# Sliding-window attention and a gated FFN on one core: two heads on half tiles of TensorE, division by block transposes, fewer and longer loads, first batch attended as a whole

## The chip, the core and the metric

One Trainium2 chip, of which the program uses one core. A core has a matrix engine (TensorE, PE in the profile, with its weight loads as PEld), a vector engine (VectorE, DVE), a scalar engine (ScalarE, ACT), GpSimd (POOL) and SyncE (SP), which here only issues transfers. Sixteen DMA engines move data between HBM and the on-chip memory SBUF. PE writes its results into PSUM: 128 partitions of eight banks, of 512 fp32 numbers each. Each engine works through its own instructions in order and waits on semaphores for the others. The metric is the device time of the program in microseconds, as the median of three runs.

## The reference

q, k and v are [4 batches, 8 heads, 768 positions, 64], fp32. Every query sees the first four keys (the sink) and the last 128 keys up to its own position. After attention the heads of a token stand side by side (512 numbers), and a gated FFN follows.

```python
scores = scale * np.matmul(q, k.transpose(0, 1, 3, 2))
keep = is_sink | in_window            # pos < 4, or 0 <= row - col < 128
scores = np.where(keep, scores, -1000000000.0)
a = np.exp(scores - max); a = a / (sum(a) + 1e-09)
x = np.matmul(a, v) -> [3072 tokens, 512]
out = (np.maximum(x @ w_gate, 0.0) * (x @ w_val)) @ w_out    # 512 -> 1536 -> 512
```

## The kernel before

All matmuls are bf16 with fp32 sums. The work of attention is cut into units: one batch and a pair of heads (four pairs p to a batch). Keys are laid out in blocks of 128: block j holds keys 124j to 124j+127, and its first four places are overwritten by the sink's keys in blocks 1, 3 and 5, so that a query finds sink and window in two or three blocks. A unit goes through these steps:

- load (L97): k, q and v by separate transfers for each head, with runs of 64 fp32 numbers (256 B).
- cast (L115): fp32 to bf16, on GpSimd except at the start.
- T (L139): six transposes of q and seven of k on PE into one PSUM tile of two banks (q in bank 0, k in bank 1). Then DVE copies q of head 0 to qz (L153), ACT copies k to kT (L154), DVE copies q of head 1 (L156). qz holds each head's q in its own 64 rows and zeros in the other 64, so that S and V can work on 128 rows.
- S (L158), for three groups G0 to G2: matmuls of kT and qz for both heads into two banks (503, 499 and 415 columns a head), Exp on ACT (L167), multiplication with a mask of ones and zeros on DVE (L168).
- V (L170), for two parts of the queries (376 and 392): matmuls of ee with vn, whose columns 64 to 127 are ones, so that row 64 of the result is the sum of the weights. ACT copies rows 0 to 64 to oab (L179).
- norm (L259): the sums go to HBM, come back spread over partitions (L269), DVE takes the reciprocal (L273), they go to HBM again and come back copied to 64 partitions (R, L279). DVE multiplies oab by R into xT (L287), which is x, transposed, in bf16.

The FFN of a block of half a batch (b, c0, n) runs in twelve chunks m (L296): four matmuls give gp, ACT takes the relu into gs (L304), four matmuls give vp, DVE multiplies both into hT (L309). gp and vp come from a pool of three single-bank tiles. ffn2 (L313) multiplies hT with wo, twelve matmuls for 128 tokens into the single-bank tile op, and ACT copies the result to ot, from where it is stored.

The order is written out by hand (L328 to L472). Of batch 0 only the first halves of the queries are attended in front (units P0), then FFN starts. A chunk with what goes with it is called a slot below: stages of attention (T, V part 1 of the unit before, S G0, S G1, S G2, V part 0), the chunk, and a share of the ffn2 matmuls that are due (f2). In the first 18 slots two stages go with a chunk, afterwards one. Loads run on SyncE's queue three units ahead. Weights come in by GpSimd's queue, cast on the way.

Waits aren't written by hand: the language puts them in from what each instruction reads and writes.

Of the kernel before, what the change touches and what calls it, by code (L numbers as in the profile page):

```python
# [14 lines left out]

QCUT = 376
# [3 lines left out]
def kernel(  # L22
# [20 lines left out]

    den_d = nc.dram_tensor("den_tmp", (B, NP, 2 * S), F32, kind="Internal").ap()
    rcp_d = nc.dram_tensor("rcp_tmp", (B, NP, 2 * S), F32, kind="Internal").ap()
# [3 lines left out]
    hpool = ctx.enter_context(tc.tile_pool(name="hp", bufs=2))  # L49
    xpool = ctx.enter_context(tc.tile_pool(name="xp", bufs=2))  # L50
    rpool = ctx.enter_context(tc.tile_pool(name="rp", bufs=2))
    dpool = ctx.enter_context(tc.tile_pool(name="dp", bufs=3))
    outpool = ctx.enter_context(tc.tile_pool(name="outp", bufs=3))
    ps_gv = ctx.enter_context(tc.tile_pool(name="ps_gv", bufs=3, space=bass.MemoryType.PSUM))
    ps_op = ctx.enter_context(tc.tile_pool(name="ps_op", bufs=1, space=bass.MemoryType.PSUM))
    ps_at = ctx.enter_context(tc.tile_pool(name="ps_at", bufs=2, space=bass.MemoryType.PSUM))


    kf = [const.tile([128, 7, 2, 64], F32, name=f"kf{i}") for i in range(2)]
    vf = [const.tile([128, 7, 2, 64], F32, name=f"vf{i}") for i in range(2)]  # L60
    qf = [const.tile([128, 6, 2, 64], F32, name=f"qf{i}") for i in range(2)]
    kn = [const.tile([128, 7, 2, 64], BF16, name=f"kn{i}") for i in range(2)]
    vn = [const.tile([128, 7, 2, 128], BF16, name=f"vn{i}") for i in range(2)]
    qn = [const.tile([128, 6, 2, 64], BF16, name=f"qn{i}") for i in range(2)]
    kT = [const.tile([128, 7, 128], BF16, name=f"kT{i}") for i in range(2)]
    qz = [const.tile([128, 2, S], BF16, name=f"qz{i}") for i in range(2)]
    ee = [const.tile([128, 3, 2, 512], BF16, name=f"ee{i}") for i in range(2)]
    oab_ = [const.tile([65, 2, S], F32, name=f"oab{i}") for i in range(4)]
    sink = const.tile([4, 2, NP, 2, 64], BF16, name="sink")
    wg = const.tile([128, KO, d_ff], BF16, name="wg")  # L70
    wv = const.tile([128, KO, d_ff], BF16, name="wv")
    wo = const.tile([128, FM, d_model], BF16, name="wo")
    ident = const.tile([128, 128], BF16, name="ident")
    msk = const.tile([128, 3, 2, 512], BF16, name="msk")

    class Unit:


        def __init__(self, i, b, p, half):
            self.i, self.b, self.p, self.half, self.s = i, b, p, half, i % 2  # L80
            if half == 0:
                self.js, self.q0, self.n, self.qn, sub = (0, 1, 2), 0, QCUT, 3, p // 2
                self.jo, self.qo, self.zo = 3 * sub, 3 * sub, 384 * sub
                self.qrows, self.qp = 384, 128
            elif half == 1:
                self.js, self.q0, self.n, self.qn = (2, 3, 4, 5, 6), QCUT, S - QCUT, 4
                self.jo, self.qo, self.zo = 0, 0, 0
                self.qrows, self.qp = S - QCUT, 98
            else:
                self.js, self.q0, self.n, self.qn = tuple(range(7)), 0, S, 6  # L90
                self.jo, self.qo, self.zo = 0, 0, 0
                self.qrows, self.qp = S, 128
            self.j5 = [j for j in self.js if j < 6]
            self.a, self.e = self.jo + self.j5[0], self.jo + self.j5[-1] + 1


        def load(self, eng=None, veng=None):  # L97
            eng, veng = eng or nc.sync, veng or eng or nc.sync
            s, a, e = self.s, self.a, self.e
            for en, x, dst in ((eng, k, kf[s]), (eng, q, qf[s]), (veng, v, vf[s])):  # L100
                for h in range(2):
                    src = x[self.b, 2 * self.p + h]
                    if x is q:
                        r = src[self.q0:self.q0 + self.qrows, :].rearrange("(p n) d -> p n d", n=self.qn)
                        en.dma_start(out=dst[0:self.qp, self.qo:self.qo + self.qn, h, :], in_=r)
                        continue
                    r = bass.AP(src.tensor, src.offset + 124 * self.j5[0] * D,
                                [[D, 128], [124 * D, e - a], [1, D]])
                    en.dma_start(out=dst[:, a:e, h, :], in_=r)  # L109
                if x is not q and 6 in self.js:  # L110
                    en.dma_start(out=dst[0:24, 6, :, :],  # L111
                                 in_=x[self.b, 2 * self.p:2 * self.p + 2, 744:768, :].rearrange("h s d -> s h d"))


        def cast(self, what, eng):  # L115
            s, a, e = self.s, self.a, self.e
            cp = eng.tensor_copy
            if what == "q":
                cp(qn[s][0:self.qp, self.qo:self.qo + self.qn, :, :].rearrange("p j h d -> p (j h d)"),  # L119
                   qf[s][0:self.qp, self.qo:self.qo + self.qn, :, :].rearrange("p j h d -> p (j h d)"))  # L120
                return
            w = 0 if what == "k" else 1
            src, dst = (kf[s], kn[s]) if w == 0 else (vf[s], vn[s])
            if w == 0:
                cp(dst[:, a:e, :, :].rearrange("p j h d -> p (j h d)"),
                   src[:, a:e, :, :].rearrange("p j h d -> p (j h d)"))
            else:
                cp(dst[:, a:e, :, 0:64], src[:, a:e, :, :])  # L128
            if 6 in self.js:
                cp(dst[0:24, 6, :, 0:64], src[0:24, 6, :, :])  # L130
            if self.half == 0:
                cp(sink[:, w, self.p, :, :], src[0:4, a, :, :])
            for j in (1, 3, 5):
                if j in self.js:
                    cp(dst[0:4, self.jo + j, :, 0:64],
                       sink[:, w, self.p, :, :] if self.half == 1 else src[0:4, self.jo, :, :])


        def T(self):  # L139
            s, nq = self.s, self.qn  # L140
            ps = ps_at.tile([128, 2, 1024], BF16, name="tps", tag="at")
            w = self.qp * nq
            po = ps[:, 0, 0:w].rearrange("d (n p) -> d n p", n=nq)
            for t in range(nq):
                nc.tensor.transpose(po[:, t, :], qn[s][0:self.qp, self.qo + t, :, :].rearrange("p h d -> p (h d)"),  # L145
                                    ident[0:self.qp, 0:self.qp])
            for j in self.js:
                nc.tensor.transpose(ps[:, 1, j * 128:(j + 1) * 128],  # L148
                                    kn[s][:, self.jo + j, :, :].rearrange("p h d -> p (h d)"), ident[:])
            z0 = self.zo + self.q0  # L150
            d0, d1 = self.js[0], self.js[-1] + 1
            zq = [qz[s][64 * h:64 * h + 64, h, z0:z0 + w].rearrange("d (p n) -> d n p", n=nq) for h in range(2)]
            nc.vector.tensor_copy(zq[0], po[0:64])  # L153
            nc.scalar.copy(kT[s][:, self.jo + d0:self.jo + d1, :].rearrange("p j n -> p (j n)"),  # L154
                           ps[:, 1, d0 * 128:d1 * 128])
            nc.vector.tensor_copy(zq[1], po[64:128])  # L156

        def S(self, g):  # L158
            s = self.s
            gi, lo, hi, segs = SEG[g]  # L160
            ps = ps_at.tile([128, 2, 512], F32, name="sps", tag="at")
            for h in range(2):
                for j, q0, c0, c1 in segs:
                    nc.tensor.matmul(out=ps[:, h, c0:c1], lhsT=kT[s][:, self.jo + j, :],  # L164
                                     rhs=qz[s][:, h, self.zo + q0:self.zo + q0 + c1 - c0], start=True, stop=True)
            x = ee[s][:, gi, :, lo:hi]
            nc.scalar.activation(x, ps[:, :, lo:hi], Act.Exp, bias=0.0, scale=scale)  # L167
            nc.vector.tensor_tensor(x, x, msk[:, gi, :, lo:hi], op=Alu.mult)  # L168

        def V(self, part, oab):  # L170
            s = self.s
            q0, n, segs = VSEG[part]
            ps = ps_at.tile([128, 2, 512], F32, name="ops", tag="at")
            for h in range(2):
                for i, (j, gi, c0, c1, o0) in enumerate(segs):
# [5 lines left out]
    def load_w(c):  # L181
        n = d_ff // 4
        for w, dst in ((moe_w_gate, wg), (moe_w_val, wv)):
            nc.gpsimd.dma_start(out=dst[:, :, c * n:(c + 1) * n],
                                in_=w.rearrange("(ko ki) n -> ki ko n", ki=128)[:, :, c * n:(c + 1) * n])
# [322 lines left out]
```

The softmax here doesn't subtract the row's maximum and nothing guards it: scores larger than these inputs give would overflow.

## Time and profile before

389.09 us (median; 388.46 to 389.14). The profiled execution has a span of 388.4 us.

| engine | busy us | share |
|---|---|---|
| PE | 272.5 | 70% |
| PEld | 163.6 | 42% |
| DVE | 207.7 | 53% |
| ACT | 141.3 | 36% |
| POOL | 83.2 | 21% |

| group | count | busy us | mean ns |
|---|---|---|---|
| L307 vp matmuls | 384 | 83.2 | 342 |
| L301 gp matmuls | 384 | 84.9 | 346 |
| L320 op matmuls | 288 | 77.3 | 384 |
| L309 hT | 96 | 51.2 | 547 |
| L153 and L156 qz | 20 + 20 | 39.8 + 40.0 | 1990, 2000 |
| L168 mask | 52 | 33.8 | 651 |
| L287 xT | 40 | 33.2 | 830 |

A matmul's mean is its time from start to end; matmuls overlap, so counts times means is more than the busy time. 96241 DMA packets move 37.74 MB, and 85692 of them are under 512 B. The rows of 40 digits in the prediction cut the span into 40 slices of 9.7 us: busy share in tenths for an engine, granted clock in tenths for PEclk. A line of the chain gives start, length and what ran. A line of waits gives the waiting engine and line, whom it waited for, the sum in us, how often, and the longest. A line of the windows gives the stretch, its length, the busy time of PE, PEld, DVE, ACT and POOL with counts of instructions, the granted clock, the busy share of the DMA engines and GB/s.

### The profile page before, as it was taken

What the parts mean: (1) busy time and instruction counts of PE and PEld (TensorE: products, weight loads), DVE (VectorE), ACT (ScalarE), POOL (GpSimd) and SP (SyncE); (2) the same over time, 40 slices, a digit from 0 to 9 for tenths busy, and PEclk for the clock granted to TensorE, in tenths of its full rate; (3) what the DMA queues carried; (4) which work ended last, traced back from release to release, by engine and by line L of the source; (5) the groups of instructions that cost most, each with busy time, mean ns of one, the idle gap of its engine ahead of it and who ended that gap; (6) DMA issues with size and microseconds to landing.
All of it is one profiled execution on the core that took longest, in us unless ns stands there. A gap on an engine that the chain in (4) does not pass through costs nothing.

```text
span 388.4 us, 5029 instructions
## 1 busy us (share of the span) xinstructions
PE 272.5 (70%) x1760; PEld 163.6 (42%) x1760; DVE 207.7 (53%) x286; ACT 141.3 (36%) x225; POOL 83.2 (21%) x203
## 2 busy tenths in 40 slices
PE   0245230176384695687498989898988999999996
PEld 0122120045252453444255555454645555555552
DVE  5661230347877767861847575767667544222220
ACT  1233120126343543531353544445363533333331
POOL 6240531307424304311404040404010000000000
PEclk9999999999887878969599999999999999999999
DMA  9957199565684554408074747291211211110002
GB/s 178 146 112 125 37 177 196 121 157 117 131 157 102 124 125 94 119 27 166 1 138 95 137 101 137 59 191 33 68 29 43 71 43 53 39 44 29 27 34 103
DMA packets 96241, 37.74 MB, mean 97 GB/s; under 512 B 85692, under 2 KB 92364, under 8 KB 96216
## 3 DMA queue, kind: packets, MB, share of 16 engines
q1 hardware_dynamic: 87208, 31.91, 37.5%
q0 software_dynamic: 5808, 4.72, 8.0%
q10 hardware_dynamic: 3200, 0.79, 1.0%
q8 instruction: 14, 0.23, 0.3%
q14 instruction: 11, 0.09, 0.1%
HBM read 35.64 MB, written 6.49 MB: 108 GB/s over the span
## 4 chain that ended last, share of the span: by engine, by line
PE 48%; DVE 24%; DMA 11%; ACT 6%; issue 4%; SPq 4%; POOL 1%; DVEq 0%; ACTq 0%; POOLq 0%
PE vp L307 14%; PE op L320 13%; PE gp L301 12%; DVE qz L153 10%; DVE qz L156 8%; PE sps L164 6%; DMA kf<-in_k_dram 4%; ACT kT L154 3%; DMA R<-rcp_tmp 3%; DMA dc<-den_tmp 2%; DVE xT L287 2%; PE ops L176 2%; ACT ee L167 2%; SPq L109 2%; SPq L111 1%
## 5 line engine op out<-in xcount | busy, mean ns | idle before, releaser
L307 PE MATMUL vp<-xT,wv 128*128 128x384 bf16 (+2 forms) x384 | 83.2, 342 | 14.2 <-ACT gs L304 14.2
L301 PE MATMUL gp<-xT,wg 128*128 128x384 bf16 (+2 forms) x384 | 84.9, 346 | 5.9 <-DVE hT L309 4.1
L320 PE MATMUL op<-wo,hT 128*128 128x512 bf16 x288 | 77.3, 384 | 0.0
L309 DVE TENSOR_TENSOR hT<-gs,vp 128x384 bf16<-128x384 f32 (+2 forms) x96 | 51.2, 547 | 43.4 <-PE vp L307 42.4
L164 PE MATMUL sps<-qz,kT 128*128 128x251 bf16 (+5 forms) x232 | 35.3, 293 | 47.8 <-DVE qz L156 39.5
L167 ACT ACTIVATE ee<-sps 128x1006 bf16<-128x1006 f32 (+4 forms) x52 | 46.1, 900 | 53.2 <-PE sps L164 53.2
L304 ACT ACTIVATE gs<-gp 128x384 f32<-128x384 f32 (+2 forms) x96 | 47.2, 492 | 41.4 <-PE gp L301 40.9
L307 PEld LDWEIGHTS <-wv 128*128 128x128 bf16 x384 | 39.2, 102 | 47.6 <-issue 25.9
L168 DVE TENSOR_TENSOR ee<-ee,msk 128x1006 bf16<-128x1006 bf16 (+4 forms) x52 | 33.8, 651 | 39.4 <-ACT ee L167 38.8
L287 DVE TENSOR_TENSOR xT<-oab,R 64x768 bf16<-64x768 f32 (+2 forms) x40 | 33.2, 830 | 34.4 <-DMA R<-rcp_tmp 34.1
L128 POOL CAST vn<-vf 128x768 bf16<-128x768 f32 (+2 forms) x20 | 14.7, 732 | 165.8 <-PE ops L176 163.1
L154 ACT COPY kT<-tps 128x896 bf16<-128x896 bf16 (+2 forms) x20 | 15.6, 778 | 95.1 <-DVE qz L153 95.1
L164 PEld LDWEIGHTS <-kT 128*128 128x128 bf16 x232 | 23.0, 113 | 63.6 <-issue 31.9
L156 DVE COPY qz<-tps 64x768 bf16<-64x768 bf16 (+2 forms) x20 | 40.0, 2000 | 17.1 <-ACT kT L154 17.1
L301 PEld LDWEIGHTS <-wg 128*128 128x128 bf16 x384 | 37.3, 103 | 27.6 <-issue 7.9
L176 PE MATMUL ops<-ee,vn 128*128 128x248 bf16 (+6 forms) x256 | 28.6, 255 | 25.8 <-DVE ee L168 18.1
L153 DVE COPY qz<-tps 64x768 bf16<-64x768 bf16 (+2 forms) x20 | 39.8, 1990 | 7.3 <-PE tps L148 7.2
L320 PEld LDWEIGHTS <-hT 128*128 128x128 bf16 x288 | 28.5, 99 | 25.9 <-issue 1.2
L176 PEld LDWEIGHTS <-vn 128*128 128x128 bf16 x256 | 22.5, 103 | 35.0 <-issue 26.5
L179 ACT COPY oab<-ops 65x752 f32<-65x752 f32 (+1 forms) x32 | 25.4, 795 | 25.5 <-PE ops L176 25.3
L145 PE MATMUL tps<-ident,qn 128*128 128x128 bf16 (+1 forms) x100 | 9.8, 236 | 18.5 <-DVE qn L119 18.3
L324 ACT COPY ot<-op 128x512 f32<-128x512 f32 x24 | 14.1, 587 | 22.2 <-PE op L320 22.2
(47 smaller groups left out, 117.9 us busy)
## 6 DMA issues: line engine op xcount, KB each, us to landing
out_dram<-ot SPq DMA_DIRECT2D x24, 256.0 KB
kf<-in_k_dram SPq DMA_DIRECT2D x24, 192.0 KB
qf<-in_q_dram SPq DMA_DIRECT2D x24, 192.0 KB
vf<-in_v_dram SPq DMA_DIRECT2D x24, 192.0 KB
R<-rcp_tmp SPq DMA_DIRECT2D x12, 384.0 KB
wg<-in_moe_w_gate_dram POOLq DMA_DIRECT2D x4, 384.0 KB, 6.3
wv<-in_moe_w_val_dram POOLq DMA_DIRECT2D x4, 384.0 KB, 8.1
wo<-in_moe_w_out_dram POOLq DMA_DIRECT2D x3, 512.0 KB, 16.3
```

The costliest lines, as they stand in the source:

```text
L153: nc.vector.tensor_copy(zq[0], po[0:64])
L156: nc.vector.tensor_copy(zq[1], po[64:128])
L164: nc.tensor.matmul(out=ps[:, h, c0:c1], lhsT=kT[s][:, self.jo + j, :], rhs=qz[s][:, h, self.zo + q0:self.zo + q0 + c1 - c0], start=True, s ...
L167: nc.scalar.activation(x, ps[:, :, lo:hi], Act.Exp, bias=0.0, scale=scale)
L168: nc.vector.tensor_tensor(x, x, msk[:, gi, :, lo:hi], op=Alu.mult)
L176: nc.tensor.matmul(out=ps[:, h, o0:o0 + c1 - c0], lhsT=vn[s][:, self.jo + j, h, :], rhs=ee[s][:, gi, h, c0:c1], start=i == 0, stop=i == le ...
L287: nc.vector.tensor_tensor(x[64 * h:64 * h + 64, p, q0:q0 + n], oab[0:64, h, q0:q0 + n], R[0][:, h, 0:n], op=Alu.mult)
L301: nc.tensor.matmul(out=gp[:, 0:n], lhsT=wg[:, ko, m * 128:(m + 1) * 128], rhs=x[:, ko, c0:c0 + n], start=ko == 0, stop=ko == KO - 1)
L304: nc.scalar.activation(gs[:, 0:n], gp[:, 0:n], Act.Relu, bias=0.0, scale=1.0)
L307: nc.tensor.matmul(out=vp[:, 0:n], lhsT=wv[:, ko, m * 128:(m + 1) * 128], rhs=x[:, ko, c0:c0 + n], start=ko == 0, stop=ko == KO - 1)
L309: nc.vector.tensor_tensor(hT[:, m, c0:c0 + n], gs[:, 0:n], vp[:, 0:n], op=Alu.mult)
L320: nc.tensor.matmul(out=op, lhsT=hTs[b][:, m, t * 128:(t + 1) * 128], rhs=wo[:, m, :], start=m == 0, stop=m == FM - 1)
```

## The change

The kernel's attention and its order are written anew; chunk and ffn2 do the same matmuls as before. Part by part:

- Loads: k and q of both heads come in one transfer each, with partition p of 96 holding eight neighbouring positions of a head (2 KB runs). v keeps 256 B runs. The weights come in fp32 into three staging buffers wst and are cast by GpSimd. All loads stand on SyncE's queue. This is to need fewer packets[...].
- T: sixteen transposes of 96 columns bring k and q to rows by head and to columns by (n, p), and the copies out of PSUM sort the columns (stride of 96 in PSUM, contiguous in SBUF): DVE 128, ACT twice 248, DVE 144 columns of k, DVE 768 of q, and a small copy of the sink. Head 0 is in rows 0 to 63, head 1 in rows 64 to 127, with no zeros.
- S: the two heads' matmuls use 64 rows each (half tiles). In the front part a matmul of the identity with mb adds -30000 to what is masked out, before Exp, in place of DVE's multiplication.
- V: each head's result goes to 64 columns of its own (half tiles); a second set of matmuls, with ones as weights, gives the sums on all 64 rows. Parts of 384 queries.
- Division: DVE transposes the sums in 32x32 blocks, takes the reciprocal of every 32nd column, transposes it back, spread, and multiplies it with the values in PSUM into xT. The way through HBM is gone.
- Buffers: PSUM is four tiles of two banks. In the front part all four rotate; later PS[2] and PS[3] serve attention, gp and vp rotate over the two halves of PS[0] and the first of PS[1], and op has the second half of PS[1].
- Order: batch 0 is attended as a whole in front. Its 24 slots then take both halves in turn for each m, with two stages a slot from slot 12 on; the 48 slots of batches 1 and 2 take one stage each, and the 24 of batch 3 none. The ffn2 matmuls of a batch run in the slots of the next one, three a slot, and those of batch 3 at the end, on three banks.

The diff, cut to its core:

```diff
-QCUT = 376
+BIG = 30000.0
+CUT = 384
...
+    PS = [pspool.tile([128, 2, 512], F32, name=f"ps{i}") for i in range(4)]
+    GV = [PS[0][:, 0, :], PS[0][:, 1, :], PS[1][:, 0, :]]
...
+    def load_kq(u):
+        for x, dst in ((k, kf[u.i % NQ]), (q, qf[u.i % NQ])):
+            nc.sync.dma_start(out=dst[0:PR, :, :],
+                              in_=x[u.b, 2 * u.p:2 * u.p + 2].rearrange("h (p n) d -> p h (n d)", n=NR))
...
+    def load_w(c, w, dst, i, o):
+        n = 256
+        nc.sync.dma_start(out=wst[i % NW][:, o:o + KO * n].rearrange("p (ko n) -> p ko n", n=n),
+                          in_=w.rearrange("(ko ki) n -> ki ko n", ki=128)[:, :, c * n:(c + 1) * n])
...
+    def T(u):
+        t = u.i % NT
+        ps = nextps()[:].bitcast(BF16)
+        for j, x in ((1, kn[u.i % 2]), (0, qn[u.i % 2])):
+            for n in range(NR):
+                nc.tensor.transpose(ps[:, j, 96 * n:96 * n + 96],
+                                    x[0:PR, n, :, :].rearrange("p h d -> p (h d)"), ident[0:PR, 0:PR])
+        vk, vq = (ps[:, j, 0:768].rearrange("d (b p) -> d p b", p=PR) for j in (1, 0))
...
+        nc.vector.tensor_copy(to(e[:, 0:128]), vk[:, 0:16])
+        for i in range(2):
+            nc.scalar.copy(to(e[:, 132 + 252 * i:380 + 252 * i]), vk[:, 16 + 31 * i:47 + 31 * i])
+        nc.vector.tensor_copy(to(e[:, 636:780]), vk[:, 78:96])
+        nc.vector.tensor_copy(to(qT[t][:]), vq)
...
+    def Sg(u, g, bias=False):
...
+        if bias:
+            for h in range(2):
+                nc.tensor.matmul(out=ps[:, h, 0:n], lhsT=ident[:], rhs=mb[:, g, 0:n], start=True, stop=False,
+                                 skip_group_check=True)
+        for x0, q0, c0, c1 in segs:
+            for h in range(2):
+                nc.tensor.matmul(out=ps[:, h, c0:c1], lhsT=kE[t][64 * h:64 * h + 64, x0:x0 + 128],
+                                 rhs=qT[t][64 * h:64 * h + 64, q0:q0 + c1 - c0], start=not bias, stop=True,
+                                 skip_group_check=True)
...
+    def V(u, part):
+        ps = nextps()
+        segs = VSEG[part]
+        for which in range(2):
+            for i, (j, g, c0, c1, o0) in enumerate(segs):
+                for h in range(2):
+                    w = vn[u.i % NV][:, j, h, :] if which == 0 else ones[:]
+                    nc.tensor.matmul(out=ps[64 * h:64 * h + 64, which, o0:o0 + c1 - c0], lhsT=w,
+                                     rhs=ee[u.i % NE][:, g, h, c0:c1], start=i == 0, stop=i == len(segs) - 1,
+                                     skip_group_check=True)
...
+        nc.vector.transpose(out=t1[:], in_=ps[:, 1, 0:CUT])
+        nc.vector.reciprocal(r[:], t1[:].rearrange("p (c e) -> p c e", e=32)[:, :, 0])
+        nc.vector.transpose(out=R[:].rearrange("p (c e) -> p c e", e=32),
+                            in_=r[:].unsqueeze(2).to_broadcast([128, CUT // 32, 32]))
+        nc.vector.tensor_tensor(xT[u.b % 2][:, u.p, CUT * part:CUT * part + CUT], ps[:, 0, 0:CUT], R[:], op=Alu.mult)
...
+        gp, vp = GV[gvn[0] % 3], GV[(gvn[0] + 1) % 3]
...
+    OP = [[PS[1][:, 1, :]], [PS[1][:, 1, :], PS[2][:, 0, :], PS[3][:, 0, :]]]
...
         for p in range(NP):
+            if p + 1 < NP:
+                head_T(U[p + 1])
+            for g in range(3):
+                Sg(U[p], g, bias=True)
+            cast_v(U[p], nc.gpsimd)
...
             if p >= 1:
+                for part in range(2):
+                    V(U[p - 1], part)
+        for c in range(6):
+            cast_w(c, wg, c, 0, nc.gpsimd)
+            cast_w(c, wv, c, 1024, nc.gpsimd)
+            if c + 3 < 6:
+                load_w(c + 3, moe_w_gate, wg, c + 3, 0)
+                load_w(c + 3, moe_w_val, wv, c + 3, 1024)
+        for part in range(2):
+            V(U[3], part)
+        for u in U[4:7]:
+            load_kq(u)
+            load_v(u)
         for c in range(3):
-            load_wo(c)
-
-
+            load_wo(c, c)
+            cast_wo(c, c, nc.gpsimd)
...
+        def first(i):
+            cast_qk(U[i], nc.gpsimd, nc.gpsimd)
+            cast_v(U[i], nc.gpsimd)
+            T(U[i])
...
+            if s < 24:
+                want.append(max(0, s - 11) * 2)
+            else:
+                want.append(min(len(stages), 24 + (s - 23)))
...
+            chunk(b, g, m)
+            while si < want[s]:
+                stages[si]()
+                si += 1
+            for _ in range(3):
+                if f2:
                     f2.popleft()()
```

## The prediction

> **What bounds the kernel now.** I read the page's engine and clock rows first, then the chain of waits in order of time, the list of waits, and the windows of 20 us.
>
> ```profile
> PE   0245230176384695687498989898988999999996
> PEclk9999999999887878969599999999999999999999
> DMA  9957199565684554408074747291211211110002
> ```
> ```profile
> 50.65 11.72 DMA kf<-in_k_dram
> 77.32 3.48 DMA R<-rcp_tmp
> ...
> 100.19 2.63 DVE qz L153
> 115.72 2.63 DVE qz L153
> 130.12 2.73 DVE qz L153
> 145.20 2.73 DVE qz L153
> ...
> 224.63 2.73 DVE qz L153
> 227.39 0.92 ACT kT L154
> 228.33 2.75 DVE qz L156
> ...
> 242.75 2.64 DVE qz L153
> 345.90 0.65 PE gp L301 x4
> 349.80 0.65 PE gp L301 x4
> ```
> ```profile
> ACT kT L154 <- DVE qz L153: 95.1, 20, 20.6
> PE sps L164 <- DVE qz L156: 39.5, 17, 5.7
> DVE qz L156 <- ACT kT L154: 17.1, 20, 1.0
> ```
> ```profile
> 0.00:20.00 20.00, 2.85 (x18) 1.88 (x18) 12.35 (x39) 3.53 (x5) 8.65 (x26) 1.00 0.89 157
> 340.00:360.00 20.00, 20.00 (x115) 11.06 (x113) 5.62 (x11) 6.09 (x12) 0.00 (x0) 1.00 0.09 33
> ```
> Four stretches. To 82 us PE is nearly idle: the chain runs over small loads and the den_tmp/rcp_tmp round trip. From 82 to about 200 two attention stages fall into a slot (one chunk plus what goes with it), and a unit takes 15 us (115.72 - 100.19, and so on)[...]. From 200 to 314 a unit takes 17.9 us (six slots). From 314 PE is full at 1.95 us a slot (two slots from 345.90 to 349.80: chunk 2 x 0.65, three op matmuls 0.65). In a unit the same three copies always stand on the chain: 2.73 + 0.92 + 2.75 = 6.4 us from PSUM to the S matmuls. The third fence says that ACT's copy, which reads the tile's second bank, waits for VectorE's reading of the first, and VectorE's second for ACT. PE does the next slot meanwhile and then idles: a unit's PE work is 6 x 1.95 + 3.1 (S and V 2 x 2834 columns, T 13 x 128, at 384 columns in 0.163 us) = 14.8 of 17.9 us.
>
> [...]the readers of two banks of one tile went one after the other, 20 times of 20.[...]
>
> **Part by part.**
> *Loads.* Runs of 256 B moved 157/0.89 = 176 GB/s of busy engines, 23 ns a packet; the 2 KB stores of the last stretch 33/0.09 = 367 GB/s, 89 ns; between them 1 KB comes to 51 ns (estimate). A unit had 4704 packets of 256 B (6.8 us over 16 engines). Now k and q are 384 of 2 KB (2.1 us), v 1584 of 256 B (2.3): 4.4 us. A weight pair is 1024 x 51/16 = 3.3 us, a third of wo 2.8. The den/rcp transfers and R's 6 MB go. One consequence is a new wait: on GpSimd the wo casts stand ahead of the casts of unit 4, and SyncE sends wo behind units 0 to 6 and all weights: 7 x 4.4 + 6 x 3.3 + 3 x 2.8 = 59 us, with start and landing 63, with casts **67 us: no T of unit 4 before**. Behind it on PE is all of FFN from slot 12.
>
> *T.* 16 transposes of 96 columns. Reading hops 192 B in PSUM, writing is contiguous: DVE 128, ACT 2 x 248, DVE 144, DVE 768 elements, one after the other if the readers stay tied. Bounds: [...]3.5 (before's strided writing, 2724/768) gives 6.0. [...]**3.4 us, from 6.4**.
>
> *Division.* Each half: [...]reciprocal 0.2 (222 ns), [...]multiplication 0.55 (as hT, 547): 1.8 us of DVE, 3.7 a unit; bounds 3.2 and 5. It replaces two xT (1.95), one reciprocal and the ACT copies of oab (1.6), and waits for no DMA. Per unit DVE has some 3.3 (T with ACT's share) + 2.0 (masks) + 3.7 + 3.3 (hT) = 12 us: below a unit's time, so not the bound with one stage a slot.
>
> *PE.* V doubles its matmuls (36; ones give the sum in 64 rows), S halves its rows. Weight loads in a tight run take about 0.055 us (seven in 0.43 at 223.99), so a concurrent pair can't take under 0.11: T 0.9 + S 7 x 0.11 + V 18 x 0.11 = 3.7 us. With no concurrency: 0.9 + 1.2 + 2.6 = 4.7. I take 4.2, and 1.0 (0 to 1.5)[...]. So attention costs PE 5.2 a unit instead of 3.1.
>
> *Steady slots.* 6 x 1.95 + 5.2 = 16.9; between T and S lie op (0.65) and a chunk (1.3), so of 3.4 us 1.4 shows: **18.3 a unit, against 17.9**: the gain on T is spent on V.
>
> *Two-stage slots* (12 to 23): before's 15 us less 3.0 (T) plus 1.5 (DVE division on the chain) = 13.5 a unit.
>
> *Head.* First T at about 7 us (setup, loads). Period by DVE: q cast 0.5, T 1.2 + 3.4, V and two divisions 4.6, about 10 us; four units and the last division: **first chunk at 45 us instead of 82**. The bias matmuls (PE) lie under the T copies, the table load that the warm activation pulls forward (1.3 us) under the first loads, the weight casts (18 on GpSimd, about 1.2 us each after 0.89 for 768 elements) under the landing of the next weights. This, not the steady state, is the gain.
>
> *Banks.* gp, vp and op were tiles of their own. Now two of the three gp/vp banks share tile PS0, and the third shares PS1 with op. If order is kept per tile, as T shows it for readers, vp waits in one slot of three for the relu of gp in the other bank (0.2 + 0.49 = 0.7 us), and in one of three op waits for hT (0.75, hidden where a stage lies between). That is 0.28 a slot with stages, 0.55 without.
>
> **The sum and the rivals.**
> A, halves tied: 45; 12 slots to 67 (with tie or wait for unit 4); four units 4 x 13.5 + 3 = 57, to 124; 48 slots 8 x 18.3 + 48 x 0.28 = 160, to 284; 24 x 2.5 = 60, to 344; last op 72 x 0.215 + 3 = 18.5: **362**. For it: three copies tied 20 times of 20. Against: those are readers; no writing into one half during reading of the other occurs in before.
> B, halves free: 67 + 54 + 146 + 47 + 18.5 = **333**.[...]
> C, slower: hopping reads at 3.5 ns add 2.6 us a unit: 4 x 2 in the head, 4 x 2.6, 8 x 2.6 = 39 onto A: **401**. For it: VectorE's strided writes did cost that.
> D: [...]pairs fully concurrent, free halves: steady units 11.7 + 3.7 + 0.4 = 15.8 (-20), the rest -8: **305**.[...]
>
> **How the numbers follow.** A 0.45, B 0.27, C 0.18, D 0.10. I predict A, 362. The range 318 to 398 holds A, B and edges of C and D. Of C nearly all is above 389.9: slower 0.18, same 0.02, faster 0.80.
>
> **What would show it.** First gp near 45 us; first T of unit 4 near 67, after the casts of wo; [...]under waits, vp for gs and op for hT with 10 us and more in total (A) or none (B); steady units of 18 to 20 us; S and V pairs that start together. Wrong if loads arrive much later than 63 us[...], or if GpSimd's casts fall behind and T waits for them in every unit.

## The result, and the profile after

The changed kernel takes **358.9 us** (median of four runs; 357.96 to 360.7), 389.12 before (four runs): a ratio of 0.923, with a 95% interval of 0.9195 to 0.9264. The forecast was 362 us. Times below are medians of all runs, while ratios leave out runs in the slower state, of which the kernels at 321.0 and 300.5 us have one each (without it 319.8 and 299.3; the trace of the first is of that run). The line numbers in this part are those of the new kernel: T's copies L178 to L183, S matmuls L196, V matmuls L213, division L219 to L223, gp L235, relu L238, vp L240, hT L242, op L255, ot L259, GpSimd's casts of k and q L111 and of wo L129.

The rows of PE and DMA, in slices of 8.9 us, on the page of the kernel after:

```profile
PE   1868287655965888898888889897989788878895
DMA  8999999399560005107230520000000000000032
```

PE is at work from the first slices on, and DMA is done with the bulk by slice 12. But PE never gets to a long row of nines, not even in the last quarter, where it was full before. The first gp matmul starts at 41.7 us; before, at 79.0 (its fourth waited until 82.0, the number that the forecast used). So the front gained 37 us, while from there to the end the new kernel takes longer: 314.6 us (356.3 - 41.7) against 309.4 (388.4 - 79.0), though it has less attention left to do. The change won once and gives back a little afterwards.

The chain of waits after, around the first T behind the front, and then at the T of three steady units:

```profile
68.48 1.04 POOL wo L129
69.52 0.98 POOL kn L111
70.50 0.99 POOL qn L111
...
71.55 0.53 PE ps L172 x8
...
73.39 0.86 DVE qT L182
...
125.66 0.70 PE ps L172 x16
144.72 0.70 PE ps L172 x16
163.28 0.70 PE ps L172 x16
```

The casts of wo stand in front of those of unit 4, as forecast. The steady units are 18.6 to 19.1 us apart (144.72 - 125.66, and so on); over seven units the mean is 18.8. The three copies of 2.73, 0.92 and 2.75 us of before are gone from the chain; q's takes 0.86 there.

The waits of PE after (engine and line, whom it waited for, us in all, times, longest):

```profile
PE ps L240 <- ACT gs L238: 20.7, 32, 0.9
PE ps L196 <- DVE qT L182: 13.8, 12, 3.3
PE ps L255 <- DVE hT L242: 8.9, 16, 0.7
...
PE ps L235 <- ACT ot L259: 4.1, 6, 0.7
PE ps L235 <- DVE hT L242: 3.5, 5, 0.7
```

PE's waits for T's last copy of q (qz L156 before, qT after) are down from 39.5 to 13.8 us. Four others now cost 37.2 us together. vp (L240) waits for the relu in 32 slots of 96, one in three: it has no use for the relu's result, and only writes into the other bank of the tile that the relu reads. The same goes for op on hT and gp on ot and hT: the hT that op multiplies is that of the batch before, and has long been done.

### The profile page after: what moved, and what is told of

It reads as the page before. It is cut to its first block, busy times and chain, and to the rows that moved or that the text cites. A ratio compares the mean times of both kernels' runs of the same rounds, so it can differ in the third digit from the quotient of the medians.

```text
span 356.3 us, 5404 instructions
## 1 busy us (share of the span) xinstructions
PE 276.0 (77%) x2114; PEld 148.3 (42%) x2136; DVE 173.6 (49%) x348; ACT 116.0 (33%) x202; POOL 71.9 (20%) x90
## 4 chain that ended last, share of the span: by engine, by line
PE 59%; DVE 16%; ACT 8%; issue 5%; DMA 5%; SPq 2%; POOL 2%; ACTq 0%; DVEq 0%; POOLq 0%
PE ps L255 17%; PE ps L240 15%; PE ps L235 14%; PE ps L213 5%; PE ps L196 4%; DVE hT L242 4%; ACT gs L238 4%; DVE qT L182 3%; PE ps L172 3%; DMA wst<-in_moe_w_out_dram 3%; DMA vf<-in_v_dram 2%; ACT kE L180 2%; ACT ot L259 2%; DVE R L221 2%; DVE t L219 2%
## 5 line engine op out<-in xcount | busy, mean ns | idle before, releaser
L242 DVE TENSOR_TENSOR hT<-gs,ps 128x384 bf16<-128x384 f32 x96 | 53.1, 553 | 104.9 <-PE ps L240 104.4
L240 PE MATMUL ps<-xT,wv 128*128 128x384 bf16 x384 | 81.9, 337 | 21.5 <-ACT gs L238 20.7
L235 PE MATMUL ps<-xT,wg 128*128 128x384 bf16 x384 | 82.6, 339 | 14.4 <-DVE xT L223 6.8
L238 ACT ACTIVATE gs<-ps 128x384 f32<-128x384 f32 x96 | 47.1, 491 | 127.3 <-PE ps L235 126.4
L255 PE MATMUL ps<-wo,hT 128*128 128x512 bf16 x266 | 71.4, 380 | 10.1 <-DVE hT L242 8.9
L240 PEld LDWEIGHTS <-wv 128*128 128x128 bf16 x384 | 38.5, 100 | 56.8 <-issue 35.9
L200 ACT ACTIVATE ee<-ps 128x1006 bf16<-128x1006 f32 (+2 forms) x48 | 45.1, 961 | 40.7 <-PE ps L196 40.7
L235 PEld LDWEIGHTS <-wg 128*128 128x128 bf16 x384 | 37.4, 100 | 50.3 <-issue 21.8
L111 POOL CAST kn<-kf 96x1024 bf16<-96x1024 f32 x16 | 16.6, 1035 | 115.8 <-PE ps L172 112.7
L255 PEld LDWEIGHTS <-hT 128*128 128x128 bf16 x288 | 25.0, 97 | 35.3 <-issue 13.9
L202 DVE TENSOR_TENSOR ee<-ee,msk 128x1006 bf16<-128x1006 bf16 (+2 forms) x36 | 25.2, 700 | 28.6 <-ACT ee L200 28.4
L196 PE MATMUL ps<-qT,kE 64*128 64x251 bf16 (+4 forms) x224 | 21.7, 281 | 16.5 <-DVE qT L182 13.8
L196 PEld LDWEIGHTS <-kE 64*128 64x128 bf16 x224 | 10.5, 101 | 35.4 <-issue 30.0
L259 ACT COPY ot<-ps 128x512 f32<-128x512 f32 x24 | 14.0, 583 | 27.3 <-PE ps L255 24.2
L219 DVE STREAM_TRANSPOSE t<-ps 128x384 f32<-128x384 f32 x32 | 18.6, 580 | 5.9 <-PE ps L213 4.8
L221 DVE STREAM_TRANSPOSE R<-r 128x384 f32<-128x384 f32 x32 | 18.5, 578 | 1.1
L223 DVE TENSOR_TENSOR xT<-ps,R 128x384 bf16<-128x384 f32 x32 | 17.8, 557 | 1.1
L213 PE MATMUL ps<-ee,vn 128*64 128x255 bf16 (+8 forms) x288 | 16.1, 236 | 0.9 <-DVE xT L223 0.9
L213 PEld LDWEIGHTS <-vn 128*64 128x64 bf16 x288 | 12.5, 110 | 7.6 <-issue 7.2
L213 PE MATMUL ps<-ee,ones 128*64 128x255 bf16 (+8 forms) x288 | 15.6, 233 | 0.0
```

Of the source, the lines that this page charges most:

```text
L196: nc.tensor.matmul(out=ps[:, h, c0:c1], lhsT=kE[t][64 * h:64 * h + 64, x0:x0 + 128], rhs=qT[t][64 * h:64 * h + 64, q0:q0 + c1 - c0], start ...
L200: nc.scalar.activation(x, ps[:, :, 0:n], Act.Exp, bias=0.0, scale=scale)
L202: nc.vector.tensor_tensor(x, x, msk[:, g, 0:n].unsqueeze(1).to_broadcast([128, 2, n]), op=Alu.mult)
L213: nc.tensor.matmul(out=ps[64 * h:64 * h + 64, which, o0:o0 + c1 - c0], lhsT=w, rhs=ee[u.i % NE][:, g, h, c0:c1], start=i == 0, stop=i == l ...
L219: nc.vector.transpose(out=t1[:], in_=ps[:, 1, 0:CUT])
L221: nc.vector.transpose(out=R[:].rearrange("p (c e) -> p c e", e=32), in_=r[:].unsqueeze(2).to_broadcast([128, CUT // 32, 32]))
```

## The experiments

Each time is beside runs of the kernel before on the same chip (389.5 to 390.0 us); a ratio is to that kernel, with its 95% interval. All but one kernel start from the changed one (0.923).

**One bank to a tile.**

```diff
-    PS = [pspool.tile([128, 2, 512], F32, name=f"ps{i}") for i in range(4)]
-    GV = [PS[0][:, 0, :], PS[0][:, 1, :], PS[1][:, 0, :]]
...                                       # PS[2], PS[3] stay; PS[0], PS[1] are given back after the front
+        headps.__exit__(None, None, None)
+        one = [single.tile([128, 512], F32, name=f"one{i}") for i in range(4)]
+        GV += [one[i][:] for i in range(3)]
+        OP += [[one[3][:]], [one[3][:], PS[2][:, 0, :], PS[3][:, 0, :]]]
```

> The changed kernel, with gp, vp and op each in a PSUM tile of one bank after the head (same seven banks of use, same order of work, same instructions). Theory (two banks of one tile are kept in order): the waits vp<-gs (20.7 us, 32 times), op<-hT (8.9) and gp<-hT (3.5) go. Of the 2.5 us of a batch 3 slot 0.5 goes (24 slots, -12), of a steady unit's 18.8 us about 2.2 (8 units, -17); slots 0 to 11 get shorter but the T of unit 4 still waits for GpSimd's casts at 70.5, so nothing there. Together 329 us (322 to 337). Rival (the ties only stand where PE would wait anyway, for ACT's relu or VectorE's queue): 355 to 360, with other waits in the place of these.

Measured: **321.0 us**, ratio 0.821 (0.817 to 0.826), 38 us less than the changed kernel. Its largest wait of PE, in the first fence, and its timeline of PE at the end of slot 11 in the second (start, length, engine, line, what; in brackets the idle time ahead and who ended it; here gp is L238, vp L243, T L175):

```profile
PE ps L175 <- POOL kn L114: 18.5, 3, 11.4
```
```profile
59.41 0.81 PE L238 MATMUL one<-xT,wg 128*128 128x384 bf16 x4
60.05 0.81 PE L243 MATMUL one<-xT,wv 128*128 128x384 bf16 x4
72.28 0.82 PE L175 MATMUL ps<-ident,kn 96*128 96x96 bf16 x8 [11.41 <-POOL kn L114]
```

No wait of vp for the relu, or of op for hT, is left. Four matmuls follow four at 0.65 us, from the first slots on. A steady unit takes 16.2 us instead of 18.8, a slot of batch 3 1.95 instead of 2.65 (in the kernel after, the gp of its first and last slot start at 273.12 and 334.12, 23 slots apart). The banks and matmuls are the same; what went is an order that is kept between the two halves of one tile. The twelve slots ahead of unit 4 got shorter for nothing: PE then stands 11.4 us for GpSimd.

**The casts of wo behind, and batch 1 spread.**

```diff
             load_wo(c, c)
-            cast_wo(c, c, nc.gpsimd)
...                                       # in first(i), ahead of T(U[i])
+            if i == 6:
+                for c in range(3):
+                    cast_wo(c, c, nc.gpsimd)
...
-                want.append(max(0, s - 11) * 2)
+                want.append(min(24, max(0, s - 3) * 6 // 5))
```

> The changed kernel, same instructions, with two placements changed: GpSimd's casts of wo stand behind the casts of units 4 to 6 instead of ahead of them, and batch 1's 24 stages are spread over slots 4 to 23 instead of two a slot over slots 12 to 23. Theory (the T of unit 4 waits only for GpSimd's queue, its data being there by about 46, and two-stage slots run at the pace of a chain, 13.5 us a unit with PE 60 to 75% busy): T of unit 4 at 49 to 53 instead of 70.6, slots 4 to 23 at 2.6 to 2.9 us each, batch 1's start at 104 to 110 instead of 125: 337 to 345 us. Rival (a unit takes its 13.5 us however it is spread, and the clock of this stretch falls further): 351 to 360.

> The untied kernel with the same two placements changed. There PE stood 11.4 us for the casts of unit 4 ahead of its T, and two-stage units took 13.4 to 14.5 us. Theory (ties, GpSimd's order and the chain of two stages a slot are three separate costs): 291 to 300 us. Rival (only the wait for the casts goes; the two-stage stretch is bound by something that moves along, clock or VectorE): 308 to 312.

Measured: with the ties **345.1 us**, ratio 0.887 (0.882 to 0.892); without them **300.5**, 0.770 (0.766 to 0.775). The first T of unit 4 came at 53.7 and 50.7 us instead of 70.6 and 72.3. 14 us of the changed kernel were GpSimd's order and the two stages a slot, and 20 of the untied one: with the ties, the costs nearly add up (38 + 14, of 58 together). Each theory came out ahead of its rival, but at the upper end of its range or just past it: 345.1 and 300.5 us where 337 to 345 and 291 to 300 were expected, and with the ties T of unit 4 at 53.7 (49 to 53) and of unit 8 at 112.0 (104 to 110). The two placements were not tried apart. In the changed kernel PE stood only 0.8 and 0.5 us for GpSimd's casts at the T of unit 4 (11.4 in the untied one), so there the order of the casts alone could bring little: it is what lets the stages start earlier.

**T one stage ahead.** On top of both:

```diff
+            if i % NP == 0:
                 order.append(stage_T(i))
...
+            if i % NP < NP - 1:
+                order.insert(len(order) - 1, stage_T(i + 1))
```

> The untied kernel with wo's casts behind and batch 1 spread, and with the T of a batch's next unit one stage earlier, ahead of the second V of the unit before it. Theory (what is left in slots 4 to 23 is PE's wait for T's copies, 2.35 us in three of four units, and some 3 us in the steady part; a slot's chunk and V are then in between): 290 to 294 us. Rival (the clock and VectorE's queue eat it: another wait of the same size on hT or xT takes its place): 298 to 302.

Measured: **289.1 us**, ratio 0.742 (0.738 to 0.745). The waits on qT were 11.0 us in the version before this; now PE's largest wait for T's copies is:

```profile
PE ps L199 <- DVE qT L185: 2.1, 3, 1.0
```

This is the fastest kernel of the study: 70 us under the changed one, with the same instructions on every engine.

**Halves: heads one after the other, and both heads on one half.**

```diff
-        for x0, q0, c0, c1 in segs:
-            for h in range(2):
+        for h in range(2):
+            for x0, q0, c0, c1 in segs:      # S; in V likewise
```
```diff
-                    nc.tensor.matmul(out=ps[64 * h:64 * h + 64, which, o0:o0 + c1 - c0], lhsT=w,
+                    nc.tensor.matmul(out=ps[0:64, which, o0:o0 + c1 - c0], lhsT=w,   # S: rows 0:64 for both heads
```

> The changed kernel, with the matmuls of the two heads in S and V issued one head after the other instead of alternating, so that no two neighbours stand on different halves of PE (but for one boundary per group). Theory (neighbours on different halves run at the same time): V's 16 and 20 matmuls go from 0.71 and 0.83 us to 1.1 and 1.3 (2572 and 3096 columns at 384 in 0.163), S gains 0.5: +1.4 us a unit on a PE that is the bound in 12 of 16 units, 371 to 380 us. Rival (the time is in the weight loads and the number of matmuls, not in concurrency): 0.71 and 0.83 stay, 357 to 361.[...]

> The changed kernel with both heads of S and V on the same half of PE: head 1's scores are computed from head 0's rows, and its V lands on head 0's 64 output rows, so head 1's attention is not computed. Same number and size of matmuls, but no two on different halves. Theory (halves run at the same time whether neighbours alternate or follow one another, which is why the kernel with heads one after the other lost only 4 us): V's 16 and 20 matmuls take 1.1 and 1.3 us instead of 0.71 and 0.83, S 1.2 instead of 0.7: 1.4 us a unit, 375 to 381 us. Rival (the pace is set by the number of matmuls, 0.044 us each, whatever half they stand on): 357 to 361.

Measured: heads one after the other 362.9 us, ratio 0.929 (0.926 to 0.933): neither theory's number. Both on one half **395.7**, 1.016 (1.012 to 1.019). The two V parts of a unit on PE, in the kernel after and then with both heads on one half:

```profile
156.02 0.81 PE L240 MATMUL ps<-xT,wv 128*128 128x384 bf16 x4
156.76 0.47 PE L213 MATMUL ps<-ee,vn 128*64 128x255 bf16 x8
157.09 0.45 PE L213 MATMUL ps<-ee,ones 128*64 128x255 bf16 x8
157.47 0.82 PE L255 MATMUL ps<-wo,hT 128*128 128x512 bf16 x2
```
```profile
162.97 0.77 PE L213 MATMUL ps<-ee,vn 128*64 128x255 bf16 x8
163.60 0.75 PE L213 MATMUL ps<-ee,ones 128*64 128x255 bf16 x8
164.28 0.82 PE L255 MATMUL ps<-wo,hT 128*128 128x512 bf16 x2
```

From the first matmul to what follows, the same sixteen take 0.71 us on two halves (157.47 - 156.76) and 1.31 on one. So the halves did run at the same time. With one head after the other they took 0.73: what came next on the free half did not have to stand next in the program (at the end of the values there, the first matmul of the sums starts at 163.33 us on one half, ahead of the last of the values, 163.38, on the other). So that order was no test of concurrency, and my expectation of 1.1 us was wrong. A steady unit went from 18.8 to 20.4 us on one half, about the 1.4 us expected. Of the 37 us in all, though, some 18 lie ahead of the first gp (59.5 instead of 41.7). PE ran at half pace there until 27 us and again from 36 to 47 (V's first sixteen matmuls took 2.4 us at 23.61, and 1.2 at 50.09), and in between it stood 7.9 us for VectorE's cast of q, which took 5.87 us instead of 0.69. Why the pace stayed low and the cast was slow isn't settled.

**k and q in 256 B runs.**

```diff
-                              in_=x[u.b, 2 * u.p:2 * u.p + 2].rearrange("h (p n) d -> p h (n d)", n=NR))
+            for h in range(2): ... in_=x[u.b, 2 * u.p + h].rearrange("(n p) d -> p n d", n=NR))
...
-        vk, vq = (ps[:, j, 0:768].rearrange("d (b p) -> d p b", p=PR) for j in (1, 0))
+        vk, vq = ps[:, 1, 0:768].rearrange("d (p b) -> d p b", b=8), ps[:, 0, 0:768]
```

> The changed kernel, with k and q loaded in runs of 256 B again (96 rows apart, one transfer a head, same queue), which brings the columns out of T in natural order, so T's copies then read PSUM without hops. Theory (loads set the head and the T of unit 4): 2.4 us more for each of seven units (from 4.4 to 6.8 by 23 ns a packet), first gp at 46 to 52 instead of 41.7, T of unit 4 at 80 to 87 instead of 71; 368 to 376 us in all. Rival (the transfers lie beside weight casts and PE work): 357 to 361. T's 768-element copy: 0.95 us as now if the hop in PSUM costs nothing, less if it does.

Measured: **356.7 us**, ratio 0.916 (0.912 to 0.920), so no slower than the changed kernel. The loads do come later: the first gp at 44.1 us (41.7), the first T of unit 4 at 77.1 (70.6), 6.5 us of the 9 to 16 expected. T paid it back. Its q copy with the hop, after, and without:

```profile
L182 DVE COPY qT<-ps x16: 947/948/949, 9.2 to 259.1; 128x768 bf16<-128x768 bf16 x16
```
```profile
L182 DVE COPY qT<-ps x16: 545/547/550, 9.6 to 260.4; 128x768 bf16<-128x768 bf16 x16
```

The hop of 192 B costs VectorE 0.40 us in 768 elements (1.23 against 0.71 ns each, fixed costs included); ScalarE's 248 took 369 ns either way. A steady unit took 18.0 us instead of 18.8. The 2 KB runs, together with the hop that they bring into T's copies, gained nothing in the end. They were one of the change's four points.

**Sorting on the read side: alone on the kernel before, and undone in the changed one.**

```diff
-        zq = [... .rearrange("d (p n) -> d n p", n=nq) for h in range(2)]       # the kernel before
+        zq = [... .rearrange("d (p n) -> d p n", n=nq) for h in range(2)]
+        po = po.rearrange("d n p -> d p n")
```
```diff
-        nc.vector.tensor_copy(to(qT[t][:]), vq)                                 # the changed kernel
+        nc.vector.tensor_copy(qT[t][:].rearrange("d (p b) -> d b p", b=8), ps[:, 0, 0:768].rearrange("d (b p) -> d b p", p=PR))
```

> The kernel before with one thing changed: the two qz copies of T read PSUM with the hop and write SBUF in order, instead of reading in order and writing with a step. Theory (the step on the write side is what made T's chain 6.4 us, and the chain stands on the path of every unit): each copy goes from 2.72 to about 0.95 us, the chain to 2.8; two-stage units from 15 to 12-12.5 (8 units), steady ones from 17.9 to 15.5-16.5 (6): 345 to 357 us, so as good as the whole change. Rival 1 (something else takes the chain's place: the round trip of den_tmp, PE itself): 372 to 386. Rival 2 (hopping reads cost what stepped writes cost): 389.

> The changed kernel with one part of it undone: T's q copy reads PSUM in order and writes SBUF with a step of 16 B (the four k copies stay sorted). Theory (a stepped write costs 3.5 ns an element, and T's copies stand on the path): the copy goes from 0.95 to about 2.7 us, and the 1.75 us show in twelve of sixteen units and partly in the head: 378 to 384 us. Rival (op and a chunk lie between T and its S matmuls, 1.95 us of PE work, so most is hidden): 359 to 366.

Measured: two lines of the kernel before alone give **364.2 us**, ratio 0.934 (0.931 to 0.938), 26 us of the whole change's 30, and with no shorter front (first gp at 77.3 instead of 79.0). The copies fell from 2.73 to 0.95 us, a steady unit from 17.7 to 15.7. It stayed 7 us above my range, and part of the gain went to another wait. The largest of PE in that kernel, V's wait for the mask, was 18.1 us in 4 waits before the edit, and five of the eight now stand in the two-stage stretch, with 8.6 us:

```profile
PE ops L177 <- DVE ee L169: 27.7, 8, 12.7
```

Undone in the changed kernel, **405.3 us**, ratio 1.040 (1.033 to 1.046): 46 us more, twice what the theory said and slower than before. The timeline of PE there, at the S matmuls of a steady unit:

```profile
150.63 0.60 PE L197 MATMUL ps<-qT,kE 64*128 64x255 bf16 x4 [2.91 <-DVE kE L184]
151.16 1.46 PE L256 MATMUL ps<-wo,hT 128*128 128x512 bf16 x3
152.42 1.40 PE L236 MATMUL ps<-xT,wg 128*128 128x384 bf16 x4
153.65 0.81 PE L241 MATMUL ps<-xT,wv 128*128 128x384 bf16 x4
```

The copy took 3.55 us, not 2.7 (4.6 ns an element at a step of 16 B; 3.5 at before's 12 B). Nearly all of the 2.6 us more show in the wait (2.91 against 0.30 and 0.26 after). And PE comes back slow: three op and four gp matmuls take 1.26 and 1.23 us from start to start, where the same seven took 0.65 and 0.66 at 145.60 us, ahead of the wait. The granted clock was 0.52 from 151.2 to 153.7 us, and 1.00 from there to 157; in the kernel after it was 1.00 from 147 to 154. A unit lost 3.7 us (22.5 against 18.8). Of the 48.5 us between the two profiled spans, 26 lie in the steady units, 10 between the T of units 4 and 8, and 11 ahead of the first gp (53.0 instead of 41.7).

**The way through HBM, for all of batch 0 and for one unit.** The sums go to den_tmp, come back, their reciprocals go to rcp_tmp and come back as R, by four transfers on ScalarE's queue:

```diff
+        if u.b == 0:              # in the second kernel: if u.i == 3
+            trip(u, part, ps, t1, R)
+            return
```

> The changed kernel with the division of batch 0 alone undone: sums go to DRAM, come back as 96 rows of 8, the reciprocals go out and come back broadcast over 64 partitions (on ScalarE's queue, each step issued one stage after the one before); batches 1 to 3 keep the block transposes. Theory (the round trip is what stood last before the first chunk in the kernel before): the first gp at 52 to 62 instead of 41.7, and the end later by what the cast-bound T of unit 4 leaves (slots 0 to 11 have about 1 us to spare): 368 to 380. Rival (the head is bound by its loads and weight casts, the round trip lies beside them): first gp at 42 to 46, 358 to 363.

> The changed kernel with the round trip through DRAM for the division of one unit alone, the last of batch 0 (both its halves; ScalarE's queue, nothing else queued behind). Tells what one trip adds where nothing stands in a line. Theory (a trip is four transfers of 2 to 7 us each, as the trips of all four units showed, against 1.95 us of VectorE): first gp at 53 to 60 instead of 41.7, the end later by that less about 1 us: 367 to 378. Rival (the trips cost only because they stood in a line for two buffers): first gp below 48, 358 to 363.

Measured: **413.6 us**, ratio 1.062 (1.057 to 1.066), with all four units; **376.4**, 0.967 (0.962 to 0.972), with one. With all, that is far above the 368 to 380 expected, and the first gp had its fourth matmul only at 102.1 us (52 to 62 expected): trips stood in a line for two buffers (ScalarE's copies wait 22.1 us for the xT that frees one) and in ScalarE's queue, where Exp stands behind the transfers, so that number is an upper end. With one, the first gp had its fourth matmul at 55.7 us, as expected, and the chain of waits shows the price (the first line is the first half's transfer, the others are the second half's):

```profile
38.93 4.97 DMA den_tmp<-R
...
45.66 2.12 DMA den_tmp<-R
...
47.87 3.68 DMA dc<-den_tmp
...
51.81 3.95 DMA rcp_tmp<-dr
...
56.32 6.19 DMA R<-rcp_tmp
...
62.64 0.57 DVE xT L238
```

24.7 us lie between the first sums (37.92) and the last xT, for what VectorE does in 3.9 (two halves of 1.95). Some 7 of them (45.66 - 38.93) are a line here too: ScalarE copies the second half only when the first half's sums have landed, because its queue already holds their next transfer. The first half alone took 17.2 us, to its xT at 55.10. The first T of unit 4 came 18 us later, the end 17.5.

## Why the prediction was right, and where it was right by luck

| step | forecast (A) | after | tiles untied |
|---|---|---|---|
| first gp, us | 45 | 41.7 | 42.5 |
| first T of unit 4 | 67 | 70.6 | 72.3 |
| first T of unit 8 | 124 | 125.5 | 128.1 |
| steady unit | 20.0 with the tie | 18.8 | 16.2 |
| slot of batch 3 | 2.5 | 2.65 | 1.95 |
| last op matmuls to the end | 18.5 | 20.0 | |

The forecast's terms add up to 362.5. With what was measured in their place the sum closes: 362.5 + 1.5 (unit 8) - 12.4 (the steady stretch, from there to the first gp of batch 3, took 147.6, not 160) + 3.2 (batch 3 took 63.2, not 60) + 1.5 (end) = 356.3, the profiled span. That 362 came so near is in part luck: errors named below cancel.

**Ties (case A against B): right.** The waits stood where and as often as forecast, one slot in three. Untied, the kernel went to 321 us, beyond B's 333. I had put 29 us on the ties; they cost 38. In the steady part it was 2.6 us a unit instead of 1.7, because there too vp's wait shows nearly in full beside stages, and in batch 3 it was 0.7 us a slot instead of 0.55: 8 x 2.6 + 24 x 0.7 = 37.6.

**Head: right, for the reason given first.** "45 instead of 82" was 41.7 instead of 79.0. One trip through HBM kept in one unit takes 17.5 us of that back. The loads' part of the argument was priced too high: by "6.8 to 4.4 us a unit", at 23 ns a packet, twice the packets should have cost the first gp 4 to 10 us and the T of unit 4 9 to 16. They cost 2.4 and 6.5, and with T's cheaper copies the end came no later.

**GpSimd's queue: right.** wo's casts ahead of unit 4's, T at 70.6. That this was not forced, and cost 14 us together with the two-stage slots, the forecast didn't see.

**Steady slots: near by luck, four terms mis-sized and partly cancelling.** PE's attention was put at 5.2 us a unit, of which 1.0 was my estimate for ten changes between full and half tiles, not shown in the trace of before, and 4.2 for T and for pairs half concurrent. On top came 1.4 for what shows of T and 1.7 for the tie. In the untied trace a unit leaves 16.2 - 6 x 1.95 = 4.5, of which 0.6 is PE's waits for T's copies. T takes 0.68 us, S about 1.0 and V 1.54. So PE's attention is 3.9 and what shows of T 0.6, and the tie was 2.6: 20.0 - 1.3 - 0.8 + 0.9 = 18.8. My estimate of 0.11 us as the floor for a pair, from two weight loads of 0.055 one after the other, did not hold (V's 18 pairs take 0.086 each). "The gain on T is spent on V" was wrong: V's pairs are cheap, and what took T's gain was the ties.

The untied trace shows some 0.1 us where a part on half tiles begins: in the steady units, vp's four matmuls take 0.65 us to the start of an op or T matmul, and 0.74 or 0.75 to that of an S or V matmul on half tiles, 32 times of 32 (in the kernel after, 156.76 - 156.02 = 0.74). In the kernel before, whose S and V use no half tiles, three op matmuls take 0.65 us whether gp, S or V follows. So of the ten changes a unit the five into half tiles take about 0.1 us each. On the way out there is less: the last eight or ten V matmuls take 0.05 to 0.07 us more than the same number before them.

**T: mechanism right, the copies put too high and their weight too low.** The copies with the sink took about 2.8 us, not 3.4. The 3.4 was my estimate, which rested on nothing that the trace of before shows; hops of 192 B measured 1.23 ns for a 2-byte element. Case C (3.5 ns for hopping reads) fell; it is the stepped write that is dear, at 3.5 to 4.6 ns an element. What I undervalued is how much T's chain costs: 26 us for two lines in the kernel before, 46 us when undone, front and slow clock included.

**Division: right.** 0.58 + 0.23 + 0.58 + 0.56 = 1.95 us a half, forecast 1.8. The two transposes in that forecast were my estimate, not shown in the trace of before.

The rivals: B's mechanism failed (the order is kept by tile, not by bank: on the same banks 358.9 us with shared tiles, 321.0 with a tile to a bank; that halves would be free was an assumption of mine, not shown in the trace of before), C's failed, and D's is close to what the untied, reordered kernels show: steady units of 15.8 forecast, 16.2 and 15.7 measured in the two fastest.

## What to carry to other kernels

In this kernel PE's waits for something whose result it didn't use were waits for a buffer (untying the tiles took 358.9 us to 321.0): look at what shares the tile, and give banks that are filled and read by turns tiles of their own. A large rewrite that moves the time little may hold several gains and a new loss of the same size; list the waits of before and after side by side and price each new one. And what stands in an in-order queue ahead of the first work of the next stage (wo's casts, which cost 14 us here together with the two-stage slots) should be what that stage needs last.

## What the runs showed of the hardware

- Matmuls on two column halves overlapped even when their heads didn't alternate: sixteen in 0.71 us alternating, 0.73 one head after the other, 1.31 on one half.
- After PE had stood still for 2.9 us, seven full matmuls behind the first four took 2.49 us instead of 1.30; the granted clock was 0.52 there.
- A change from full to half tiles took some 0.1 us (0.74 or 0.75 us instead of 0.65 for the four matmuls ahead of it).
- A step of 16 B in SBUF writes cost VectorE 3.55 us for 768 bf16 elements; sorting by a hop of 192 B in PSUM reads 0.95; neither 0.55.
